# Moving two first-half transposes of tile 2 one gate tile sooner in the matmul stream of tile 1

## The chip, the cores and the metric

The kernel runs on one core of a Trainium2 chip. The metric is device microseconds of one execution, the median of several. The profiler's span runs from the first to the last instruction and is about 1.75 us shorter than the time. PE is TensorE, ACT is ScalarE, DVE is VectorE; PEld is TensorE's weight loads, SPq the queue that issues DMA transfers. PSUM is the memory that matmuls write, in banks; an eviction is the copy of a result out of it. The first 512-column matmul is always that of the gate; the 512-column warm-up matmuls before it, on constants, are not meant.

## The reference, cut to what matters

```python
x = A_x                                   # (1, 2048, 512) bf16
xn = _layernorm(x, axis=-1)
return x + _A_ref(xn, ...) + _B_ref(xn, w_gate, w_up, w_down)

def _B_ref(x, w_gate, w_up, w_down):      # the part that matters here
    g = _silu(x @ w_gate)                 # w_gate: 512 x 1376
    u = x @ w_up
    return (g * u) @ w_down
# _A_ref: a diagonal linear recurrence over the 2048 rows; its first step
# multiplies xn by a complex matrix B (real part B_re, imaginary part B_im).
```

The 2048 rows are worked in four chunks of 512 rows, each of four tiles of 128 rows. The change touches the very first stage: chunk 0, tiles 0 to 3, against the first seven 128-column tiles of `w_gate`.

## The kernel before

Every operation is a task with an engine, the tasks that it depends on, and an estimate. A list scheduler orders DVE, ACT and POOL; PE and the DMA queue keep the order of the program text. In the first stage the layernorm of each tile is made in halves, TensorE transposes each half, ScalarE (VectorE for tile 3) copies it out of PSUM, and the gate matmuls of this tile follow at once. All transposes share one PSUM bank, `slot`, so each pair must wait until the copy of the pair before it is done.

```python
def xt_tile_fine(a, h, slot=None):         # tile a, half h
    ...
    def tr2(e):                            # two 128x128 transposes
        for j in range(2):
            kt = h * 2 + j
            inst = e.transpose(out=ptr[:, slot, j * 128:(j + 1) * 128],
                               in_=xn_sb[:, a % NXN, kt * 128:(kt + 1) * 128], identity=ident[:])
        return inst
    g.add("pe", tr2, reads=[("xh", a, h), ("ident",)], writes=BK(slot), name="xT%d_%d" % (a, h), ...)
    ... # a == 3: one DVE copy; h == 0: two ACT copies of 128 columns; else one ACT copy of 256

def ffn_gate_quarters(pairs):
    ...
    place = {(0, 2, 4): (1, 0), (1, 0, 2): (1, 1), (1, 2, 2): (2, 0), (2, 0, 2): (2, 1), (2, 2, 1): (3, 0), (3, 0, 1): (3, 1)}
    for q in range(4):                     # tile of 128 rows
        for k0, k1 in (...)[q]:            # parts of the sum over k
            for n, (i, bk) in enumerate(tiles):   # seven gate tiles
                if (q, k0, n) in place:
                    xt_tile_fine(*place[(q, k0, n)])
                ... # (k1 - k0) matmuls of 128 x 128 x 128
    ...
    ffn_mm(0, NQ, "g", xt_pair[0])         # the eighth gate tile, 512 columns
```

Of the kernel before, what the change touches and what calls it, by code (L numbers as in the profile page):

```python
# [249 lines left out]
def bass_parallel_sum__ssm_conv_s5__swiglu_ffn__prompt_kernel(  # L250
# [32 lines left out]
    with es:  # L283
# [90 lines left out]
        def next_pair():  # L374
            for _ in range(NB // 2):
                b = 2 * (pair_ctr[0] % (NB // 2))
                pair_ctr[0] += 1
                if not (b in reserved or _bank_live(b) or _bank_live(b + 1)):
                    return b
            raise AssertionError("all PSUM pairs live")  # L380
# [4 lines left out]
        def BK(b):  # L385
            return [("bk", b, 0), ("bk", b, 1)]
# [79 lines left out]
        def act_table(func, order):  # L466
            g.add("act", lambda e: e.activation(out=sm[:, NSM - 1, 0:1], in_=epst[:], func=func, bias=epst[:, 0:1]), reads=[("epst",)], writes=[("sm", "_warm")],
                  name="act_warm", est=1500, order=order)
# [3 lines left out]
        def pe_warm(n, w=512, bk=None):  # L472
            if bk is None:
                bk = next_pair()

            def mm(e, bk=bk):
                for _ in range(n):
                    inst = e.matmul(pbank[:, bk, 0:w], lhsT=one.to_broadcast([128, 128]), rhs=one.to_broadcast([128, w]), start=True, stop=True)
                return inst
            g.add("pe", mm, writes=BK(bk), name="pe_warm", est=n * w * 0.84, ninst=n)  # L480
# [96 lines left out]
        def xt_tile_fine(a, h, slot=None):  # L577
            slot = xt_pair[0] if slot is None else slot

            def tr2(e):  # L580
# [5 lines that stand above are left out]
            g.add("pe", tr2, reads=[("xh", a, h), ("ident",)], writes=BK(slot), name="xT%d_%d" % (a, h), est=2 * 64, ninst=2)  # L586
            dst, src = xnT[0][:, a % 4, 2 * h:2 * h + 2, :], ptr[:, slot, 0:256].rearrange("p (k t) -> p k t", k=2)
            wr = [("xnTq", a, 2 * h + j) for j in range(2)] + ([("xnT", 0, a % 4)] if h else [])
            if a == 3:
                t = g.add("dve", lambda e: e.tensor_copy(out=dst, in_=src), reads=BK(slot), writes=wr, name="xTev%d_%d" % (a, h), est=320, order=(hold["xn3"],))  # L590
            elif h == 0:
                for j in range(2):
                    t = g.add("act", lambda e, j=j: e.activation(out=dst[:, j], in_=src[:, j], func=AF.Identity), reads=BK(slot), writes=wr[j:j + 1],
                              name="xTev%d_0%d" % (a, j), est=240, order=(t,) if j else ())
                    if j == 0:
                        hold["ev%da" % a] = t
            else:
                t = g.add("act", lambda e: e.activation(out=dst, in_=src, func=AF.Identity), reads=BK(slot), writes=wr, name="xTev%d_%d" % (a, h), est=340)
            hold["ev%d%d" % (a, h)] = t
# [154 lines left out]
        def ffn_mm(c, i, which, bk):  # L754
            fs = fsz[i]
            w = wg if which == "g" else wu

            def mm(e, bk=bk, w=w, i=i, fs=fs, c=c):
                for kt in range(KT):
                    inst = e.matmul(pbank[0:fs, bk, :].rearrange("p (j t) -> p j t", j=4), lhsT=w[:, kt, i * 128:i * 128 + fs], rhs=xnT[c][:, :, kt, :],  # L760
                                    start=(kt == 0), stop=(kt == KT - 1))
                return inst
            g.add("pe", mm, reads=wres("wg" if which == "g" else "wu", i) + [("xnT", c, j) for j in range(4)],
                  writes=BK(bk), name="mm_%s%d_%d" % (which, c, i), est=4 * 216, ninst=4)

        def silu_pair(c, ip, bk):
            i0, n = FP[ip]
            rows = slice(0, 128)
            sl = gctr[0] % NG
            gctr[0] += 1  # L770
            sg_slot[(c, ip)] = sl
            g.add("act", lambda e: e.activation(out=sg[rows, sl, 0:n, :].rearrange("p a t -> p (a t)"), in_=pair_f32(rows, bk, 512 * n), func=AF.Silu),  # L772
                  reads=sum([BK(bk + k) for k in range(n)], []), writes=[("sg", sl)], name="silu%d_%d" % (c, ip), est=63 + 427 * n)
# [8 lines left out]
        def ffn_gate_quarters(pairs):  # L782
            banks = {ip: next_pair() for ip in pairs}
            reserved.update(banks.values())
            tiles = [(2 * ip + k, banks[ip] + k) for ip in pairs for k in range(2)]
            xt_pair[0] = tiles.pop()[1]
            wbank = tiles[-1][1]
            pe_warm(9, 512, wbank)
            pe_warm(2, 128, wbank)
            ln_chunk0()  # L790
            xt_tile_fine(0, 0, wbank)
            pe_warm(1, 256, tiles[-2][1])
            xt_tile_fine(0, 1)
            pe_warm(1, 256, tiles[-2][1])
            place = {(0, 2, 4): (1, 0), (1, 0, 2): (1, 1), (1, 2, 2): (2, 0), (2, 0, 2): (2, 1), (2, 2, 1): (3, 0), (3, 0, 1): (3, 1)}
            for q in range(4):
                for k0, k1 in (((0, 1), (1, 2), (2, 3), (3, 4)), ((0, 1), (1, 2), (2, 4)), ((0, 1), (1, 2), (2, 4)), ((0, 2), (2, 4)))[q]:
                    for n, (i, bk) in enumerate(tiles):
                        if (q, k0, n) in place:
                            xt_tile_fine(*place[(q, k0, n)])  # L800

                        def mm(e, bk=bk, i=i, q=q, k0=k0, k1=k1):
                            for kt in range(k0, k1):
                                inst = e.matmul(pbank[:, bk, q * 128:(q + 1) * 128], lhsT=wg[:, kt, i * 128:(i + 1) * 128], rhs=xnT[0][:, q, kt, :],
                                                start=(kt == 0), stop=(kt == KT - 1))
                            return inst
                        g.add("pe", mm, reads=[("wg", "a%d" % max(k - 1, 0)) for k in range(k0, k1)] + [("xnTq", q, k) for k in range(k0, k1)], writes=BK(bk),
                              name="mm_gq%d_%d_%d" % (i, q, k0), est=(k1 - k0) * 56, ninst=k1 - k0)
            reserved.clear()
            seq = ["sd0", "negm0", "nmr0", "xa01", "ev0a", "ev00", "sd1", "ev01", "ev1a", "ev10", "sd2", "ev11", "ev2a", "ev20", "sd3", "ev21"]  # L810
            for a_, b_ in zip(seq, seq[1:]):
                hold[b_].od.add(hold[a_])
            act_table(AF.Silu, (hold["ev21"],))
            hold["evac"] = g.tasks[-1]
            ffn_mm(0, NQ, "g", xt_pair[0])
            for ip in pairs:
                silu_pair(0, ip, banks[ip])
            hold["evac"] = [t for t in g.tasks if t.name == "silu0_0"][0]
# [128 lines left out]
        def dc_chunk(c, mid=None, split_last=False):  # L947
# [22 lines left out]
            for (lt, c0, nc_), bk in zip(items, banks):  # L970
# [14 lines left out]
                if nc_ == 128 and c0 == 256:  # L985
# [3 lines left out]
                    reads=[("xo", a, c) for c in ((256, 384) if nc_ == 128 else (c0,))], out_=True)  # L989

        ffn_gate_quarters([0, 1, 2, 3])
        params_a()
        tables()
# [104 lines left out]
```

## Time and profile before

| | before |
|---|---|
| time, median of 3 (range) | 178.9 us (178.81 to 179.25) |
| span of the profile | 177.2 us |
| busy: PE, DVE, ACT | 98%, 92%, 49% |
| first 128-column gate matmul starts | 5.80 us |
| first 512-column matmul starts | 12.88 us |

The page of the kernel before: instruction counts, and the chain that ended last by engine.

```profile
PE 173.5 (98%) x927; PEld 84.1 (47%) x935; DVE 162.7 (92%) x284; ACT 87.4 (49%) x116; POOL 11.1 (6%) x22
...
PE 60%; DMA 17%; DVE 15%; SPq 3%; issue 1%; POOL 1%; ACT 1%
...
L964 PE MATMUL pb<-wd,hT 128*128 128x512 bf16 (+2 forms) x176 | 34.5, 355 | 0.3 <-ACT uf L868 0.2
```

The page lists PE with 60% of the chain, and a wait of PE of 0.2 us for a ScalarE eviction (line 868) near 67 us.

The timeline of PE around the change (start us, duration us, engine, line; line 583 is a transpose, line 804 a gate matmul):

```profile
8.35 0.44 PE L804 MATMUL pb<-xnT,wg 128*128 128x128 bf16 x5
8.63 0.28 PE L583 MATMUL pb<-ident,xn_sb 128*128 128x128 bf16 x2
8.74 0.83 PE L804 MATMUL pb<-xnT,wg 128*128 128x128 bf16 x12
9.53 0.27 PE L583 MATMUL pb<-ident,xn_sb 128*128 128x128 bf16 x2
```

Ends are modelled and overlap the next start, so go by starts. Twelve matmuls 56 ns apart take 0.67 us, but 9.53 - 8.74 is 0.79: PE stood 0.12 us ahead of the second-half transposes of tile 2. ScalarE's timeline shows for what:

```profile
8.95 0.45 ACT L593 ACTIVATE xnT<-pb 128x128 bf16<-128x128 bf16 x2 [0.62 <-PE pb L583]
```

The two copies of the first half, which free the bank, end at 9.39 us.

### The profile page before, as it was taken

The page shows a single profiled execution, that of the slowest core. Times are in us where ns is not written, and L with a number is a line of the kernel's source. Part 1 is how long each engine was busy: PE and PEld are TensorE (multiplying, and loading weights), DVE is VectorE, ACT ScalarE, POOL GpSimd, SP SyncE. Part 2 cuts the span into 40 slices and gives each one's busy share as a digit, 9 for nine tenths or more (in the row PEclk, how much of TensorE's full clock was granted, in tenths as well). Part 3 has the DMA queues.
Part 4 walks back from the last instruction along what each step waited for, and adds up shares of the span by engine and source line. Part 5 has one row for each costly group of instructions (what it writes and reads, how often), then busy time and mean ns, then how long its engine had stood idle before and what let it go on. Part 6 is the DMA issues. An engine that isn't in the chain of part 4 may idle for free.

```text
span 177.2 us, 2418 instructions
## 1 busy us (share of the span) xinstructions
PE 173.5 (98%) x927; PEld 84.1 (47%) x935; DVE 162.7 (92%) x284; ACT 87.4 (49%) x116; POOL 11.1 (6%) x22
## 2 busy tenths in 40 slices
PE   8999999999999999999999999999999999999994
PEld 2894444444444444444444444444444444444644
DVE  2965999899899999999999999999999999999943
ACT  4679989989979779220456554000365520000000
POOL 3040500050050000000000000000000000000000
DMA  5892777662567500002000000001100000000032
GB/s 167 273 372 81 122 129 112 171 143 70 142 130 269 113 7 0 0 4 89 31 0 0 0 0 4 0 0 59 59 0 4 0 0 0 0 0 32 31 110 68
DMA packets 22966, 12.37 MB, mean 70 GB/s; under 512 B 15180, under 2 KB 22956, under 8 KB 22956
## 3 DMA queue, kind: packets, MB, share of 16 engines
q1 hardware_dynamic: 22652, 11.77, 25.3%
q10 hardware_dynamic: 304, 0.46, 0.8%
q8 instruction: 7, 0.11, 0.3%
q14 instruction: 3, 0.02, 0.0%
HBM read 6.46 MB, written 2.10 MB: 48 GB/s over the span
## 4 chain that ended last, share of the span: by engine, by line
PE 60%; DMA 17%; DVE 15%; SPq 3%; issue 1%; POOL 1%; ACT 1%
PE pb L760 19%; PE pb L964 19%; PE pb L978 16%; DMA x_sb<-in_A_x_dram 7%; DVE rot L921 4%; PE pb L881 4%; SPq L405 3%; DVE st L483 3%; DMA xnT<-xn_sb 3%; DMA hss<-in_A_C_im_dram 3%; DVE rot L912 3%; DMA hss<-in_A_C_re_dram 2%; DMA dsk<-in_A_Dskip_dram 2%; PE pb L975 2%; DVE hT L832 2%
## 5 line engine op out<-in xcount | busy, mean ns | idle before, releaser
L921 DVE TENSOR_TENSOR_SCAN rot<-sm,car,rot 128x512 bf16<-128x512 f32 x32 | 38.9, 1266 | 0.0
L772 ACT ACTIVATE sg<-pb 128x1024 bf16<-128x1024 f32 x20 | 20.1, 1021 | 32.5 <-PE pb L760 31.8
L964 PE MATMUL pb<-wd,hT 128*128 128x512 bf16 (+2 forms) x176 | 34.5, 355 | 0.3 <-ACT uf L868 0.2
L978 PE MATMUL pb<-W,hss 128*128 128x512 bf16 (+2 forms) x140 | 29.7, 355 | 0.2
L760 PE MATMUL pb<-xnT,wu 128*128 128x512 bf16 x120 | 27.9, 379 | 0.0
L964 PEld LDWEIGHTS pb<-wd,hT 128*128 128x128 bf16 x180 | 16.8, 98 | 18.2 <-issue 0.4
L830 ACT ACTIVATE uf<-pb 128x1024 bf16<-128x1024 f32 x20 | 20.5, 1024 | 8.3 <-PE pb L760 8.0
L760 PE MATMUL pb<-xnT,wg 128*128 128x512 bf16 x92 | 21.8, 380 | 0.0
L881 PE MATMUL pb<-xnT,BT 128*128 128x512 bf16 x96 | 21.0, 380 | 0.0
L978 PEld LDWEIGHTS pb<-W,hss 128*128 128x128 bf16 x144 | 13.5, 97 | 14.4
L888 ACT ACTIVATE u_sb<-pb 128x1024 bf16<-128x1024 f32 x16 | 16.2, 1019 | 4.6 <-PE pb L881 4.6
L760 PEld LDWEIGHTS pb<-xnT,wu 128*128 128x128 bf16 x120 | 11.7, 98 | 14.2 <-issue 0.2
L881 PEld LDWEIGHTS pb<-xnT,BT 128*128 128x128 bf16 x96 | 9.4, 98 | 11.3 <-DMA BT<-in_A_B_im_dram 0.2
L983 DVE TENSOR_TENSOR x_sb<-pb,x_sb 128x512 bf16<-128x512 f32 (+2 forms) x18 | 11.1, 629 | 3.6 <-PE pb L978 3.0
L760 PEld LDWEIGHTS pb<-xnT,wg 128*128 128x128 bf16 x92 | 9.0, 98 | 10.6
L832 DVE TENSOR_TENSOR hT<-sg,uf 128x1024 bf16<-128x1024 bf16 x20 | 13.4, 681 | 0.3 <-ACT uf L830 0.3
L912 DVE TENSOR_TENSOR rot<-u_sb,cosT 128x2048 bf16<-128x2048 bf16 x8 | 9.7, 1218 | 0.1
L912 DVE TENSOR_TENSOR rot<-rot,sin 128x2048 bf16<-128x2048 bf16 x8 | 9.8, 1220 | 0.0
L912 DVE TENSOR_TENSOR rot<-u_sb,sin 128x2048 bf16<-128x2048 bf16 x8 | 9.7, 1217 | 0.0
L912 DVE TENSOR_TENSOR rot<-rot,cosT 128x2048 bf16<-128x2048 bf16 x8 | 9.7, 1215 | 0.0
L483 DVE BATCH_NORM_STATS2 st<-x_sb 128x6 f32<-128x512 bf16 x12 | 7.4, 680 | 2.4 <-DMA x_sb<-in_A_x_dram 2.4
L912 DVE TENSOR_TENSOR rot<-rot 128x2048 bf16<-128x2048 bf16 x8 | 9.6, 1217 | 0.0
(93 smaller groups left out, 180.9 us busy)
## 6 DMA issues: line engine op xcount, KB each, us to landing
out_dram<-x_sb SPq DMA_DIRECT2D x15, 128.0 KB, 1.7
x_sb<-in_A_x_dram SPq DMA_DIRECT2D x3, 512.0 KB, 4.7
wd<-in_B_w_down_dram SPq DMA_DIRECT2D x1, 1280.0 KB, 7.2
wu<-in_B_w_up_dram SPq DMA_DIRECT2D x1, 768.0 KB, 4.8
wu<-in_B_w_up_dram SPq DMA_DIRECT2D x1, 608.0 KB, 6.9
x_sb<-in_A_x_dram SPq DMA_DIRECT2D x4, 128.0 KB, 3.1
wg<-in_B_w_gate_dram SPq DMA_DIRECT2D x1, 480.0 KB, 5.8
wg<-in_B_w_gate_dram ACTq DMA_DIRECT2D x1, 448.0 KB, 3.8
```

The source lines that it names most:

```text
L483: return g.add("dve", lambda e, a=a: e.bn_stats(out=st[:, a % 8, :], in_=x_sb[:, a, :]), reads=[("x", a)], writes=[("st", a % 8), ("st0", ...
L760: inst = e.matmul(pbank[0:fs, bk, :].rearrange("p (j t) -> p j t", j=4), lhsT=w[:, kt, i * 128:i * 128 + fs], rhs=xnT[c][:, :, kt, :], sta ...
L772: g.add("act", lambda e: e.activation(out=sg[rows, sl, 0:n, :].rearrange("p a t -> p (a t)"), in_=pair_f32(rows, bk, 512 * n), func=AF.Sil ...
L830: g.add("act", lambda e: e.activation(out=uf[rows, ul, 0:n, :].rearrange("p a t -> p (a t)"), in_=pair_f32(rows, bk, 512 * n), func=AF.Ide ...
L832: g.add("dve", lambda e: e.tensor_tensor(out=hT[rows, hb, i0:i0 + n, :], in0=sg[rows, sl, 0:n, :], in1=uf[rows, ul, 0:n, :], op=ALU.mult), ...
L881: inst = e.matmul(pbank[:, bk, :].rearrange("p (j t) -> p j t", j=4), lhsT=BT[:, ri, kt, pt * 128:(pt + 1) * 128], rhs=xnT[c][:, :, kt, :] ...
L888: g.add("act", lambda e: e.activation(out=u_sb[:, us].rearrange("p r t -> p (r t)"), in_=pair_f32(slice(0, 128), b0), func=AF.Identity), r ...
L912: tt = lambda out, a, b, op, r, w, nm: g.add("dve", lambda e: e.tensor_tensor(out=out, in0=a, in1=b, op=op), reads=r, writes=w, name="%s_% ...
L921: g.add("dve", lambda e, A0=A0, A1=A1, k=k, ri=ri, pt=pt: e.tensor_tensor_scan(out=A1[:, k, ri, :], data0=rr[:, pt:pt + 1].to_broadcast([1 ...
L964: inst = e.matmul(pbank[:, bk, 0:nc_], lhsT=hT[0:fs, hb, i, lt * 128:(lt + 1) * 128], rhs=wd[0:fs, i, c0:c0 + nc_], start=(i == 0), stop=F ...
L978: inst = e.matmul(pbank[:, bk, 0:nc_], lhsT=hss[:, hb, pt, ri, lt * 128:(lt + 1) * 128], rhs=W12[:, ri, pt, c0:c0 + nc_], start=False, sto ...
L983: g.add("dve", lambda e, bk=bk, a=a, c0=c0, nc_=nc_: e.tensor_tensor(out=x_sb[:, a, c0:c0 + nc_], in0=pbank[:, bk, 0:nc_], in1=x_sb[:, a, ...
```

## The change

The intent is to start the first-half transposes of tile 2 one gate tile (two matmuls) sooner, so that the copies end sooner and the second half need not wait.

```diff
-place = {..., (1, 0, 2): (1, 1), (1, 2, 2): (2, 0), (2, 0, 2): (2, 1), ...}
+place = {..., (1, 0, 2): (1, 1), (1, 2, 1): (2, 0), (2, 0, 2): (2, 1), ...}
```

Two matmuls move from before to behind these transposes on PE. All other engines keep their order.

More of the change, by code (lines that the diff above doesn't have):

```diff
@@ L794, in ffn_gate_quarters @@
             pe_warm(1, 256, tiles[-2][1])
-            place = {(0, 2, 4): (1, 0), (1, 0, 2): (1, 1), (1, 2, 2): (2, 0), (2, 0, 2): (2, 1), (2, 2, 1): (3, 0), (3, 0, 1): (3, 1)}
+            place = {(0, 2, 4): (1, 0), (1, 0, 2): (1, 1), (1, 2, 1): (2, 0), (2, 0, 2): (2, 1), (2, 2, 1): (3, 0), (3, 0, 1): (3, 1)}
             for q in range(4):
```

## The prediction

> **What bounds the kernel now.** The page gives a span of 177.2 us, PE busy 98%, DVE 92%, granted clock 1.000. The chain that ended last has two parts. From 67.7 us to the end it is the matmul stream, almost without gaps. Before that it never touches PE: it is the DMA queue's serial chain (x tiles 4-7 landed 15.98; B transposes issued 16.03 and 20.50; first transpose of xn 24.84; x tiles 8-11 29.57; C transposes 32.84 and 36.92; Dskip 41.58, landed about 45.3), then VectorE without a gap from 45.32 to 66.2. ScalarE then does one 0.72 us step for W and the eviction L868 (67.01 to 67.60), and PE waits 0.16 us for that before the matmul at 67.71 (view of waits, PE). This is the join that decides.
>
> **What the change does.** The orders of DVE, ACT, POOL and SP are unchanged; on PE two matmuls (one gate tile) move from before to behind the two first-half transposes of tile 2. Nothing is added or removed. In the trace matmuls of this stage start 56 ns apart (the Trainium skill, "TensorE: Matmul & The Clock Gate", section "Back-to-back issue gap", gives N/2.4 + 2.5, so 56 for N = 128; the trace agrees). So these transposes come 112 ns sooner: weight load at 8.466 instead of 8.578 us.
>
> Can they? They read the normalized half that VectorE finished at 8.373, and reuse the PSUM bank that ScalarE released at 8.322. Hand-overs here take 40 to 56 ns (an eviction ended 7.556, the waiting weight load started 7.612). Ready at about 8.42 to 8.43: margin some 40 ns, so no new wait, narrowly.
>
> What it buys: the two ScalarE evictions of that half (8.945 to 9.390) free the bank for the second-half transposes of tile 2. Their place in the stream stays, and there the matmul starts are 176 ns apart (9.358 to 9.534): a stall of 120 ns. With the evictions 112 ns sooner (ScalarE has been free since 8.322) it falls to about 10 ns. It is the only sizeable stall among the gate quarters. So that stage should end about 0.11 us sooner: first 512-column matmul at 12.77 instead of 12.88 us. Tile 3 follows with no new wait: its first half was ready at 10.15 and is wanted at about 10.26.
>
> **On the critical path?** I think not. PE then runs without waits to 67 us and arrives at the join 0.11 us sooner, where it waits for a ScalarE/VectorE chain that goes back to DMA landings, which depend on no matmul of this stage. So the wait at 67.7 should grow from 0.16 to about 0.27 us and the end stay. If that chain has slack that I can't see, at most 0.11 us (0.06%) arrives. Both lie inside the spread of the runs (178.81 to 179.25).
>
> **Prediction.** 178.85 us, range 178.55 to 179.2. Chances: faster by over 2% 0.003, within 2% 0.994, slower by over 2% 0.003.
>
> **What would show it.** Right: the first-half transposes of tile 2 at about 8.47, the gap before the second-half ones shrunk from 176 ns to under 75, first 512-column matmul about 12.77, PE's wait for the L868 eviction grown by about 0.11. Wrong: a new gap before the first-half transposes; or a PE gain that survives past 68 us.
>
> **What would make it wrong.** The 40 ns margin: if VectorE's half comes later in another run, PE stalls by the difference, though that too should vanish at the join. DMA landing times scatter from run to run, and as they carry the first part of the chain, a shift of 0.1 to 0.3 us from them would hide any effect of the change.

## More of the kernel before

How waits reach the engine matters as well:

```python
deps = set(after)                          # an unordered set of task objects
...
for d in t.deps:
    ...
    waits[k] = (d.sem, d.lvl)
t.waits = list(waits.values())             # so their order is not fixed by the text
...
for sem, val in t.waits:
    eng_obj.wait_ge(sem, val)
inst = t.fn(eng_obj)
```

One wait can ride on the instruction itself; a second one becomes a separate wait instruction ahead of it. In the trace of before, the wait for ScalarE ahead of the second half of tile 2 is such an instruction, 51 ns long, at 9.427 us, and the weight load that follows starts at 9.503.

Note the counts: 927 matmuls stand against 935 weight loads, and line 964 shows 176 matmuls.

## The result

| | before | after |
|---|---|---|
| time, median of 6 (range) | 178.95 us (178.81 to 179.25) | 178.98 us (178.84 to 179.41) |
| ratio | | 1.0006, 95% interval 0.9991 to 1.0021 |
| span of the profile | 177.2 us | 177.1 us |
| first 512-column matmul | 12.88 us | 12.73 us |

The ratio is the mean time of one kernel's runs over that of the other's of the same rounds, so not quite the ratio of the medians quoted.

The lines of the page of the kernel after that answer to those above:

```profile
PE 173.7 (98%) x935; PEld 84.1 (47%) x935; DVE 162.6 (92%) x284; ACT 87.3 (49%) x116; POOL 11.1 (6%) x22
...
PE 96%; DMA 1%; DVE 1%; ACT 1%; issue 0%; ACTq 0%
...
L964 PE MATMUL pb<-wd,hT 128*128 128x512 bf16 (+2 forms) x180 | 35.2, 355 | 0.0
```

PE and ACT around the change, kernel after:

```profile
8.48 0.28 PE L583 MATMUL pb<-ident,xn_sb 128*128 128x128 bf16 x2
8.60 0.94 PE L804 MATMUL pb<-xnT,wg 128*128 128x128 bf16 x14
9.39 0.27 PE L583 MATMUL pb<-ident,xn_sb 128*128 128x128 bf16 x2
```

```profile
8.80 0.45 ACT L593 ACTIVATE xnT<-pb 128x128 bf16<-128x128 bf16 x2 [0.51 <-PE pb L583]
```

Now fourteen matmuls stand between, 14 x 56 is 0.78 us, and 9.39 - 8.60 is 0.79: the 0.12 us stall is down to about 0.01. That is the predicted local effect. But two things contradict the rest of my account:

1. The chain of waits is now 96% PE, and the wait near 67 us, which I called the join that decides, is not there. From the first 512-column matmul to the last matmul it is 161.787 us before and 161.785 us after: what PE has gained at 12.7 us it still has at the end.
2. The gate stage (first gate matmul to first 512-column matmul) became only 0.036 us shorter, 7.081 to 7.045, not 0.11. In this profile the matmul starts ahead of the second-half transposes of tile 1, which stand before anything that moved, are 176 ns apart instead of 86.

For the first point the weight loads near 67 us are the witness. They show the same picture in both kernels. PEld, before, then after:

```profile
66.96 0.11 PEld L853 LDWEIGHTS pb<-xnT,wu 128*64 128x64 bf16 x1
67.48 0.55 PEld L964 LDWEIGHTS pb<-wd,hT 128*128 128x128 bf16 x4 [0.41 <-issue]
```

```profile
66.81 0.11 PEld L853 LDWEIGHTS pb<-xnT,wu 128*64 128x64 bf16 x1
67.34 0.55 PEld L964 LDWEIGHTS pb<-wd,hT 128*128 128x128 bf16 x4 [0.41 <-ACT scrC L728]
```

PE, before, then after:

```profile
67.17 0.38 PE L853 MATMUL pb<-xnT,wu 128*64 128x512 bf16 x1
67.71 0.59 PE L964 MATMUL pb<-wd,hT 128*128 128x512 bf16 x2 [0.16 <-ACT uf L868]
```

```profile
67.03 0.38 PE L853 MATMUL pb<-xnT,wu 128*64 128x512 bf16 x1
67.34 0.82 PE L964 MATMUL pb<-wd,hT 128*128 128x512 bf16 x3
```

Before, the weight load starts at 67.48, but the first matmul shown starts at 67.71; after, both start at 67.34. The step from the last matmul of line 853 to the first one shown of line 964 is 0.54 us in each of the nine profiles of this document whose counts are short, and 0.31 us in each of the four whose counts are complete. The profile of before has seven more such steps, of 0.43 to 0.44 us, twice the usual 0.216: with this one, eight steps for eight missing records. In the kernel before, the record of the first matmul of line 964 is missing. The hole looks like a wait, the profile names a releaser for it (the ScalarE eviction ended at 67.60), and from there the chain runs off into VectorE and DMA. In the profile of after that eviction ended only at 67.716, when the matmuls of line 964 had been running since 67.34: PE does not wait for it.

### The profile page after: what moved, and what is told of

The parts are those of the page before. It is cut to its first block, busy times and chain, and to the rows that moved or that the text cites. A ratio compares the mean times of both kernels' runs of the same rounds, so it can differ in the third digit from the quotient of the medians. Undisturbed runs are those within 1.5% of the kernel's fastest.

```text
span 177.1 us, 2426 instructions
## 1 busy us (share of the span) xinstructions
PE 173.7 (98%) x935; PEld 84.1 (47%) x935; DVE 162.6 (92%) x284; ACT 87.3 (49%) x116; POOL 11.1 (6%) x22
## 4 chain that ended last, share of the span: by engine, by line
PE 96%; DMA 1%; DVE 1%; ACT 1%; issue 0%; ACTq 0%
PE pb L760 36%; PE pb L964 20%; PE pb L978 16%; PE pb L881 16%; PE pb L804 4%; PE pb L975 2%; PE pb L843 2%; DMA x_sb<-in_A_x_dram 1%; PE pb L853 1%; PE pb L583 1%; DVE st L531 0%; ACT xn_sb L549 0%; ACT sd L525 0%; ACT nm L546 0%; DVE x_sb L983 0%
## 5 line engine op out<-in xcount | busy, mean ns | idle before, releaser
L964 PE MATMUL pb<-wd,hT 128*128 128x512 bf16 (+2 forms) x180 | 35.2, 355 | 0.0
L978 PE MATMUL pb<-W,hss 128*128 128x512 bf16 (+2 forms) x144 | 30.3, 355 | 0.0
```

The costliest lines, as they stand in the source:

```text
L964: inst = e.matmul(pbank[:, bk, 0:nc_], lhsT=hT[0:fs, hb, i, lt * 128:(lt + 1) * 128], rhs=wd[0:fs, i, c0:c0 + nc_], start=(i == 0), stop=F ...
L978: inst = e.matmul(pbank[:, bk, 0:nc_], lhsT=hss[:, hb, pt, ri, lt * 128:(lt + 1) * 128], rhs=W12[:, ri, pt, c0:c0 + nc_], start=False, sto ...
```

## The experiments

The theory now: PE is the limit from the gate stage to the end; what the gate stage gains arrives in full; the tile-1 stall in the profile after came from which of two waits became the separate instruction, which the program text leaves open. Rivals: a join near 67 us that takes the gain (the prediction), and a change that itself lengthens the tile-1 stall.

### Fixing the order of the two waits: b_slow, b_fast, a_slow, a_fast

The kernels of before (b) and after (a) with one line changed, so that the waits have a fixed order. In "fast" ScalarE's wait rides on the transpose's weight load and VectorE's is the separate instruction; in "slow" it is the reverse, for the second halves of tiles 1 and 2. The rest is identical between fast and slow.

```diff
-t.waits = list(waits.values())
+t.waits = sorted(waits.values(), key=lambda w: (-1 if t.name in ("xT0_0",) else 1)
+    * [id(eng_sems[e]) for e in ("pool", "pe", "dve", "act")].index(id(w[0]))
+    if any(w[0] is s for s in eng_sems.values()) else -9)       # slow
+# fast: the same with t.name in ("xT0_0", "xT1_1", "xT2_1")
```

> Kernel of before; the order of the two semaphore waits of the second-half transposes of tiles 1 and 2 is fixed so that the wait for ScalarE is the separate wait instruction (VectorE's rides on the weight load). Theory 'wait order' (the 90 ns that the after profile lost at the second-half transposes of tile 1 came from which wait was put where, not from the change): matmul starts 176 ns apart before both second-half transposes (tile 1 and tile 2), gate stage from its first 128-column matmul to the first 512-column one about 7.16 us. Rival 'the change itself lengthened the tile-1 stall': 86 ns before tile 1, 176 before tile 2, stage 7.08 us. From the first 512-column matmul to the last matmul 161.79 us under the theory that PE runs through (nothing absorbed).

> Kernel of before; the wait for ScalarE rides on the weight load, VectorE's is the separate instruction. Theory 'wait order': 86 ns before tile 1's and about 86 before tile 2's second-half transposes, gate stage about 7.00 us, 0.16 us less than b_slow. Rival (order does not matter): same stage as b_slow within 0.02. If PE runs through, time 0.16 us below b_slow; if the old idea of a join near 67 us holds, times equal and the PE wait there grows by 0.16.

> Kernel of after, waits ordered as in b_slow. Theory 'wait order': 176 ns before tile 1's, about 64 before tile 2's second-half transposes, gate stage about 7.05 us, 0.11 us less than b_slow: this is the change alone. Rival 'the change lengthens the tile-1 stall': b_slow would show 86 there while a_slow shows 176. Time about 0.11 us below b_slow if PE runs through, equal if absorbed.

> Kernel of after, waits ordered as in b_fast. Theory 'wait order': 86 ns before tile 1's, 56 before tile 2's, gate stage about 6.96 us, 0.20 us less than b_slow and only about 0.04 less than b_fast: with good wait order the change is worth little. Time at best 0.20 us below b_slow; a part may be lost where PE first uses the second transposed B matrix near 24.8 us, whose landing left PE only about 0.1 us in the two profiles at hand.

Measured (step: distance of the matmul starts ahead of the second-half transposes, unstalled 56 ns; rest: first 512-column matmul to last matmul; times are medians of 6, and those of the kernel before on the same chip had a median of 179.09):

| | step, tile 1 | step, tile 2 | gate stage | rest | time | ratio to before, 95% |
|---|---|---|---|---|---|---|
| b_slow | 176 ns | 175 ns | 7.242 us | 161.787 us | 179.21 us | 1.0012 (0.9998 to 1.0025) |
| b_fast | 56 | 85 | 7.102 | 161.787 | 178.81 | 0.9992 (0.9979 to 1.0006) |
| a_slow | 175 | 63 | 7.513 | 161.786 | 178.87 | 0.9999 (0.9984 to 1.0014) |
| a_fast | 86 | 56 | 6.965 | 161.784 | 178.93 | 0.9997 (0.9984 to 1.0011) |

The step of tile 1 in a_slow, then in a_fast (PE):

```profile
7.38 0.83 PE L804 MATMUL pb<-xnT,wg 128*128 128x128 bf16 x12
8.16 0.27 PE L583 MATMUL pb<-ident,xn_sb 128*128 128x128 bf16 x2
```

```profile
6.86 0.83 PE L804 MATMUL pb<-xnT,wg 128*128 128x128 bf16 x12
7.56 0.28 PE L583 MATMUL pb<-ident,xn_sb 128*128 128x128 bf16 x2
```

Twelve matmuls take 0.67 us; the starts are 0.78 us apart in slow and 0.70 in fast.

The steps settle the wait order: slow costs 90 ns where PE really waits (86 against 176), with either kernel, so the change does not lengthen the tile-1 stall. The change alone is worth 112 ns at tile 2 with the slow order (175 to 63) and 29 ns with the fast one (85 to 56). The tile-1 step of b_fast is 56 rather than 86 because PE came later there, by the two weight waits told below.

The stage totals missed my numbers in three of four, because other things happened in these single executions. In a_slow the gate matmuls started with nine steps of 106 or 107 ns, about 0.46 us more than nine of 56. In b_fast two gate matmuls came after steps of 120 and 112 ns: parts of `w_gate` had landed at 6.461 and 7.031, and the weight loads that waited for them started 42 and 41 ns later. In b_slow the excess of 0.08 us is mostly a step of 120 ns ahead of the first-half transposes of tile 1, whose half VectorE finished late because the rows of x of tile 1 had landed late (VectorE waited 0.7 us for them). There the first gate matmul itself also had to wait for its weights, which delays the start of the stage, at 6.105 us, and not its length (view of waits, PEld: total us, times, longest us):

```profile
PEld pb L804 <- DMA wg<-in_B_w_gate_dram: 0.7, 1, 0.7
```

The 107 ns steps fit the cold clock of the Trainium skill, "TensorE: Matmul & The Clock Gate", section "What's actually happening": the window that releases the full clock is free-running, so the release comes at a different time in each run. In the trace's clock records the full clock began 4.58 us after the first instruction in the profile of after and 6.77 us after it in a_slow. That the window is free-running no run here shows. The long steps end where such a record begins: the last one at 6.751 in a_slow, 14 ns before it, and 8 and 20 ns before it in the two kernels below that have them. No interval of the times tells one of these four kernels from before: 0.1 us is 0.06%, and the intervals are 0.3% wide.

### Shorter and longer gate stages: a_fast_minus, a_fast_minus_lift, a_fast_plus

To see where a larger gain or loss goes, I took 14 matmuls (0.78 us) out of the gate stage of a_fast (wrong result: quarter 3 sums only half of k), or put 14 in (correct result, they write a bank that is then overwritten). The third kernel is minus, with the first users of B_im reading B_re instead (also wrong, same stream). The scheduler's estimates were adjusted so that the engine orders stay (in the minus kernels one VectorE instruction moved).

```diff
 # a_fast_minus
-((0, 2), (2, 4)))[q]                 # quarter 3: both halves of k
+((0, 2),))[q]                        # the first half alone, with stop=(kt == 1)
 # a_fast_minus_lift, in addition
-lhsT=BT[:, ri, kt, ...]              # and the same in reads=
+lhsT=BT[:, (ri if c or pt > 1 else 0), kt, ...]
 # a_fast_plus
+pe_warm(14, 128, xt_pair[0])         # 14 matmuls of 128 columns
 ffn_mm(0, NQ, "g", xt_pair[0])
```

> Kernel a_fast, but quarter 3 of the gate tiles does only half of its sum over k: 14 matmuls of 128 columns less (0.78 us), wrong result on purpose. Where does a larger gain of PE in the gate stage end up? Stage about 6.18 us in all theories. Old idea (join near 67 us): new PE gap of about 0.8 us near 67 us, none before, time as a_fast. 'PE runs through': no gap, 161.79 us from first 512-column matmul to last matmul, time 0.78 us below a_fast. 'Runs through up to the landing of the second transposed B matrix': PE would want it at about 24.0 us, it landed between 24.34 and 24.77 in six profiles, so a gap of 0.4 to 0.8 us at the fifth B matmul, and only 0 to 0.4 us of the 0.78 arrive.

> As a_fast_minus, and the first eight imaginary-part B matmuls of chunk 0 take the real-part matrix, which landed 4 us earlier (wrong result on purpose, same matmuls and same orders on all engines). If the landing of the second B matrix is the limit and nothing else is within 0.8 us: no gap, 161.79 us from first 512-column matmul to last matmul, time about 0.78 us (0.44%) below a_fast. If there is a join near 67 us: gap of about 0.8 us there and time as a_fast.

> As a_fast, with 14 more 128-column matmuls (0.78 us) into a bank that is then overwritten, right before the last gate tile; result correct. PE runs through: stage 7.75 us, 161.79 from there to the last matmul, time 0.78 us (0.44%) above a_fast. Join near 67 us with PE waiting there: less than the full 0.78 arrives.

Medians are of 4 runs; the kernel before had 179.17 us in these rounds.

| | gate stage | rest | time | ratio to before, 95% |
|---|---|---|---|---|
| a_fast_minus | 6.494 us | 162.086 us | 178.71 us | 0.9974 (0.9957 to 0.9991) |
| a_fast_minus_lift | 6.400 | 161.786 | 178.17 | 0.9943 (0.9928 to 0.9958) |
| a_fast_plus | 7.801 | 161.782 | 179.62 | 1.0024 (1.0009 to 1.0039) |

There is no join near 67 us: with plus and with minus_lift the rest is the same to 5 ns, although PE reached the place 1.3 us apart. What looks like a wait there is the same in both, because both have the missing record (views of waits, PE, of minus_lift, then of plus):

```profile
PE pb L964 <- ACT scrC L728: 0.2, 1, 0.2
```

```profile
PE pb L964 <- issue: 0.2, 1, 0.2
```

From the start of the last matmul to the end of the span it is 2.58 to 2.60 us in all 13 profiles, so what PE has gained there does reach the end. The times agree: minus_lift and plus, from the same rounds, differ by 28 matmuls, 1.57 us, and their medians by 1.45 us; their intervals lie clear of each other.

The gain does meet a limit, but a different one and much sooner. Weight loads of a_fast_minus near 24 us:

```profile
23.31 0.74 PEld L881 LDWEIGHTS pb<-xnT,BT 128*128 128x128 bf16 x4
24.67 1.41 PEld L881 LDWEIGHTS pb<-xnT,BT 128*128 128x128 bf16 x8 [0.62 <-DMA BT<-in_A_B_im_dram]
```

and the same place in a_fast_minus_lift:

```profile
23.24 2.69 PEld L881 LDWEIGHTS pb<-xnT,BT 128*128 128x128 bf16 x13
```

PE wanted the transposed B_im before it had landed (24.63 us) and lost 0.29 us (matmul starts 506 ns apart instead of 216); the rest grew by 0.30 us. With B_re in its place the wait is gone and the rest is 161.786 again. The stages of both minus kernels were 0.2 to 0.3 us longer than the 6.18 that I expected, again from matmul steps of 106 or 107 ns at the start (six and four of them, about 50 ns each). So the 0.29 us is a lower figure: this execution of a_fast_minus had already lost 0.31 us to its cold start, and without that PE would have waited about 0.6 us for the same landing (an estimate from these two numbers), which leaves about 0.2 of the 0.78. The times say the same: against a_two below (178.92, same rounds, 14 matmuls more, gate stage 0.05 us longer than that of a_fast) a_fast_minus is 0.21 us faster and minus_lift 0.75, though 0.21 is within the scatter. That is inside the 0 to 0.4 that I expected.

### One more gate tile sooner: a_two

```diff
-(1, 2, 1): (2, 0)
+(1, 2, 0): (2, 0)
```

> As a_fast, with the first-half transposes of tile 2 one more gate tile sooner (before the first gate tile of that group). They would be wanted about 112 ns sooner still, while VectorE's half and the bank come free only 40 to 100 ns before they are used now: a new gap, matmul starts 75 to 130 ns apart before them instead of 56; second-half transposes of tile 2 at 56. Stage 0 to 0.07 us longer than a_fast, no gain. If the margin were larger than I read: 56 apart, stage unchanged.

Measured: time 178.92 us (ratio 0.9985, 0.9970 to 1.0000; median of 4), rest 161.786, gate stage 7.017 us against 6.965 of a_fast. The step ahead of the first-half transposes is now 114 ns instead of 56; tile 2's second half has 56. Timeline of PE:

```profile
7.65 0.83 PE L804 MATMUL pb<-xnT,wg 128*128 128x128 bf16 x12
8.38 0.27 PE L583 MATMUL pb<-ident,xn_sb 128*128 128x128 bf16 x2
8.49 1.05 PE L804 MATMUL pb<-xnT,wg 128*128 128x128 bf16 x16
9.38 0.28 PE L583 MATMUL pb<-ident,xn_sb 128*128 128x128 bf16 x2
```

The waiting weight load started at 8.350, 53 ns after VectorE had finished the half at 8.297. The same hand-over in a_fast would have allowed 8.373, and it started at 8.414: the margin is 41 ns, as the prediction had it. A VectorE hand-over of 52 ns is seen alone in b_slow (half done at 7.129, weight load at 7.181). In a_two the transposes also got a separate wait for ScalarE, in the slow order, and its copy, done at 8.235, would by the 113 ns that such a wait took in after (7.451 to 7.564) have held the weight load to 8.348; so a_two does not tell which of the two ended last. The margin is not safe in each execution either: in a_fast_plus, with the changed place as in a_fast, VectorE finished at 8.379 and the step there was 62 ns. The changed place is the last one of the three tried without a stall worth the name.

### The unchanged kernels, built again: before_again_1, before_again_2, after_again_1

> The unchanged kernel of before, built again. The program collects an instruction's waits from an unordered set, so where the ScalarE wait ends up may differ from build to build. If so: matmul starts before the second-half transposes of tiles 1 and 2 are each about 86 (or 56, if PE was late for another reason) or about 176 ns apart, in a combination that need not be the 86 and 176 of the first profile. If builds are identical: 86 and 176 again. In either case 161.79 us from first 512-column matmul to last matmul.

> As before_again_1: a third build of the same kernel. Build lottery: combination may differ again; identical builds: 86 and 176. 161.79 us from first 512-column matmul to last matmul.

> The unchanged kernel of after, built again. Build lottery: before the second-half transposes of tile 1 either about 86 or about 176 ns, of tile 2 either 56 or about 64 ns. Identical builds: 176 and 64 again. 161.79 us from first 512-column matmul to last matmul.

| | step, tile 1 | step, tile 2 | gate stage | rest | time of the profiled run |
|---|---|---|---|---|---|
| before (first profile) | 86 ns | 176 ns | 7.081 us | 161.787 us | 179.0 us |
| before_again_1 | 86 | 175 | 7.079 | 161.787 | 178.89 |
| before_again_2 | 87 | 176 | 7.081 | 161.828 | 178.88 |
| after (first profile) | 176 | 64 | 7.045 | 161.785 | 178.84 |
| after_again_1 | 88 | 64 | 6.970 | 161.787 | 178.73 |

The build of after did come out differently: tile 1 at 88 ns this time. The trace shows why: the separate wait instruction ahead of the second half of tile 1 is for ScalarE in the first profile of after and for VectorE in after_again_1. The three builds of before agree, with VectorE's separate at tile 1 and ScalarE's at tile 2. Set against them, after_again_1 has the same tile-1 step, and its gate stage is shorter by 0.11 us, exactly the predicted amount, all of it at tile 2. PE in after_again_1:

```profile
8.38 0.28 PE L583 MATMUL pb<-ident,xn_sb 128*128 128x128 bf16 x2
8.49 0.94 PE L804 MATMUL pb<-xnT,wg 128*128 128x128 bf16 x14
9.28 0.27 PE L583 MATMUL pb<-ident,xn_sb 128*128 128x128 bf16 x2
```

before_again_1 also had a complete record near 67 us. Its page, with the instruction counts, the chain and line 964:

```profile
PE 173.3 (98%) x935; PEld 83.9 (47%) x935; DVE 162.5 (92%) x284; ACT 87.5 (49%) x116; POOL 11.1 (6%) x22
...
PE 96%; DMA 1%; DVE 1%; ACT 1%; issue 0%; ACTq 0%
...
L964 PE MATMUL pb<-wd,hT 128*128 128x512 bf16 (+2 forms) x180 | 35.2, 355 | 0.0
```

The same program, so the 60% chain of the first profile was an artefact of the hole. before_again_2 shows the B_im limit at its edge: there B_im landed at 24.81 us, its first matmul came 248 ns after the one before instead of 216, and the rest is 0.04 us longer.

## Why the prediction was right or wrong, point by point

- **Time: right.** 178.98 us against 178.85 (178.55 to 179.2). It was right because the effect, however accounted, is about 0.1 us, below the scatter. Both the join (nothing arrives) and the true account (0.11 us arrives) lie inside the range, so the hit is luck as far as the join goes.
- **The stall and its size: right.** 120 ns ahead of the second-half transposes of tile 2 fell to 8 ns (176 to 64), and with the same wait order at tile 1 the gate stage shrank from 7.081 to 6.970 us, as predicted 0.11.
- **No new wait at the first half, narrowly: right.** The hand-over measured in a_two makes the margin 41 ns, and in a_fast_plus it was used up by 6 ns. (The eviction that the prediction puts at 7.556 ended at 7.562.)
- **First 512-column matmul 0.11 us sooner: right in mechanism, not in that profile.** 12.77 predicted, 12.73 measured, but the sum was different: the stage started 0.11 us sooner, gained 0.11 at tile 2, and lost 0.09 at tile 1 because that build had its waits in the slow order. I had taken the tile-1 step for a property of the program; it is one of the build.
- **"On the critical path? I think not": wrong.** The step that failed is "PE ... arrives at the join 0.11 us sooner, where it waits for a ScalarE/VectorE chain". There is no such wait: PE's time from 12.88 us to the last matmul, 161.787 us, is 161.785 after. I read a missing matmul record as one. The rest was 161.78 to 161.79 us in 11 of 13 profiles, with gate stages from 6.40 to 7.80 us, and the two exceptions are both at the landing of B_im. So the gain does get past 68 us, which I had listed as a sign that I was wrong.
- **Where the gain went in the times:** it was not absorbed; it lies under scatter of the same size or larger: the build's wait order (0.09 us per pair of transposes), the late full clock (about 0.46 us in a_slow), the weights' landing (b_slow, b_fast). That the times gain 0.06% is not shown by them; only the profiles show it, and the times only for the seven times larger changes of plus and minus_lift. What is argued, not shown, is how often B_im lands late enough to take part of the gain: one of five profiles of the two unchanged kernels had such a wait, of 0.03 us at that matmul.

The better version that the experiments suggest is a_fast: the change plus fixed waits. Its gate stage was 6.965 us, 0.005 below after_again_1 and 0.12 below before. It was timed in five rounds and is not told from before (0.9997). Giving the transposes other columns of the same bank I did not try: the Trainium skill, "PSUM — Partial Sum Buffer", section "PSUM bank collisions raise a hardware error", says that a TensorE write and a ScalarE read at the same time collide in one bank and quadrant of partitions even at disjoint columns. No run here shows it.

## What to carry to other kernels

Before a gap in a matmul stream is called a wait, compare the counts of weight loads and matmuls, and the step with that of a profile whose counts agree: here 0.54 us against 0.31. That a weight load starts 0.2 us ahead of its matmul proves nothing by itself; in the 512-column streams here it often does (a_fast: 23.720 and 23.934). A chain of waits built on such a hole can be wrong for half the kernel. For effects below the scatter of times, compare intervals within the profile (here the rest, which repeated to 5 ns in 11 of 13 profiles, and the stage, to 2 ns in three of before where no cold clock or late landing touched it), and profile each kernel more than once. If an instruction waits for two engines, let the wait that ends last ride on the instruction itself (worth 90 ns here), and do not leave the order to an unordered set.

## What the Trainium skill lacked or had wrong

- "TensorE: Matmul & The Clock Gate", section "Back-to-back issue gap", says that a stream of weight load and matmul pairs sustains about 81 ns per matmul at N = 128 and 131 at N = 512. Here every gate matmul has its own weight load and the starts are 56 ns apart, and those of 512 columns 215 to 217 ns apart: the formula that the section calls isolated, which the prediction used without saying so, holds in the stream.
- "Perfetto Trace Analysis", section "Identifying Dependency Chains", says that an instruction which waits for several engines may get separate wait instructions ahead of it, but not what this costs. Here, with the late wait on the separate instruction (51 ns long), the transposes started 144 ns after the copy had ended (after, tile 1: 7.451 to 7.595), with the late wait on the weight load 54 ns after (before, tile 1: 7.562 to 7.616).
- The same page does not warn that matmul records can be missing. In nine of the 13 profiles eight are (927 matmuls against 935 weight loads in before; 176 of 180 of line 964 and 140 of 144 of line 978). In most of the nine the chain of waits came out right all the same; in the first profile of before it fell from 96% PE to 60%.
